# Block sums of a weight matrix: accumulating transfers or VectorE, with a new order of steps

## The chip, the cores and the metric

The kernel runs on one core of one Trainium2 chip. A core has five engines: TensorE (PE in the profile; PEld is its loading of weights), VectorE (DVE), ScalarE (ACT), GpSimd (POOL) and SyncE (SP). Each takes its instructions in order, and they wait for each other by semaphores. SyncE here does nothing but issue transfers (DMA), ScalarE and GpSimd issue some too. The metric is the device time of one execution in microseconds, from repeated runs; the profile comes from one further execution.

## The reference

```python
mod = (_silu(c) @ w_mod).reshape(c.shape[0], 6, 1, -1)
sa, ca, ga, sb, cb, gb = (mod[:, 0], mod[:, 1], mod[:, 2], mod[:, 3], mod[:, 4], mod[:, 5])
h = _layernorm(x, axis=-1) * (1 + ca) + sa
x = x + ga * _A_ref(h, A_w_r, A_w_i)      # irfft2(rfft2(h) * (w_r + 1j * w_i))
h = _layernorm(x, axis=-1) * (1 + cb) + sb
x = x + gb * _B_ref(h, B_w1, B_b1, B_w2)  # mish(h @ w1 + b1) @ w2
```

x is 2048 rows of 512 (float32); w1 is 512 x 1376, w2 is 1376 x 512. The two-dimensional spectral filter (A) comes first, then the dense layer (B).

## The kernel before

The Fourier transforms are products with constant matrices. The forward transform and the filter take up the first part of the program; its order is written out in loops and isn't touched. The change is in the second part, which holds the last transform back to rows (p3_col and p3_row, 16 each, with the addition to x on VectorE at L821) and the dense layer. In this part every piece of work is a *step*: a small function that issues a few instructions. Each step is entered with a key (`plan.at(key, fn, *args)`), the steps are sorted by key and so get a number, and the long string `ORDER` says in which order the numbered steps are issued. There is no scheduler beyond it: each engine gets its instructions in the order in which the steps issue them.

Matrix products of the dense layer are made in parts of lower precision: each operand is split into a high part (a copy with rounding, on ACT) and a low part (the difference, on DVE), and TensorE makes three products of 128x256 for each pair of blocks. For w1 this is `split_w1` (L726 high part, L727 low part).

w1 is taken in block columns t = 1 to 5 of 256 columns each (and a rest of 96, `single_w1`). A block column has four quarters A11, A12, A21, A22, each two k-blocks of 128x128, so 128 partitions x 256 elements. For the first group of 512 rows (i = 0) the products are made plainly from the four quarters (`up`, set PLAIN). For the later three groups (i = 1 to 3) seven products replace eight (a Strassen-Winograd scheme): they need, beside A11, A12 and A22, four sums:

- S1 = A21 + A22
- S3 = A11 - A21
- S2 = A11 - S1
- S4 = A12 + S2

so S2 needs S1, and S4 needs S2. The right operands are sums T1 to T4 of blocks of the activations (`sum_in`, `split_in`). The seven products are named 1 to 7; `up` makes one (L920), `evict` or `plain_evict` (L929) takes it from the bank to SBUF, and `down` (L1023) and its kin multiply by w2 (split at L855, L856).

For each t the raw block column comes by `load_w1` (L716) into `src[t]`, a slot shared with T1 (odd t) or T2 (even t). `block_w1` splits a quarter into a slot of a ring of eight (tile wr), `keep_w1` stores the split to DRAM (L735), and `fetch_w1` (L723) brings it back into the ring for the later row groups. `sum_w1` makes the four sums, in stages called steps 0, 1 and 2:

- S1: step 0 copies A21 from DRAM (L749, SyncE), step 1 adds A22 by an accumulating transfer issued by GpSimd (L752), step 2 splits it and stores the split.
- S3: step 0 negates A21 from `src[t]` (L745, ACT) and adds A11 by an accumulating transfer; step 2 splits and stores.
- S2: step 0 negates S1 in place (L747, ACT) and adds A11 by an accumulating transfer; step 2 splits and stores.
- S4: step 1 adds A12 to S2 by an accumulating transfer; step 2 splits and stores.

The tiles in which sums stand are slots shared with T4 (`temps[0]`), or `wsum` for t = 3; the splits of sums stand in two halves of the slot of T3 before they are stored. The profile calls all of these shared slots hT. SyncE's queue holds, in the order of the steps, the loads of w1 and w2 (L844), the stores of splits, the fetches, and loads for the modulation vector (L619).

Of the kernel before, what the change touches and what calls it, by code (L numbers as in the profile page):

```python
# [10 lines left out]
ALU = mybir.AluOpType  # L11
# [20 lines left out]
POOL_LOW = range(1, 15, 2)  # L32

ORDER = (
# [44 lines left out]
)  # L79


# [1 line left out]
def tile_spectral_block(ctx: ExitStack, tc: tile.TileContext, x_d, w1_d, b1_d, w2_d,  # L83
                        c_d, xt_d, wm_d, wq_d, wz_d, kr_d, km_d, kc_d, ki_d, kf_d, kv_d, kw_d, kp_d, out_d):
    nc = tc.nc
# [615 lines left out]
    ring, raws, src, temps, stage = {}, {}, {}, {}, {}  # L701
# [7 lines left out]
    def w1_block(t, a, v=None):  # L709
        j, i = int(a[1]) - 1, int(a[2]) - 1  # L710
        at = P * j + (256 * t - 256 if v is None else 0)
        return (w1v if v is None else v)[:, 2 * i:2 * i + 2, at:at + P]
# [24 lines left out]
    def sum_w1(t, a, step):  # L737
        if not temps:
            temps[0] = shared("T4").rearrange("p (n k f) -> p n k f", n=4, k=2)
            temps[1] = wsum.rearrange("p (n k f) -> p n k f", n=2, k=2)  # L740
            stage[0] = shared("T3", F32R).rearrange("p (n i k f) -> p n i k f", n=2, i=2, k=2)
        v = temps[1][:, a == "S3"] if t % 3 == 0 else temps[0][:, 2 * (t % 3 - 1) + (a == "S3")]
        if step == 0:
            if a == "S3":
                nc.scalar.mul(v, w1_block(t, "A21", src[t]), -1.0)  # L745
            if a == "S2":
                nc.scalar.mul(v, v, -1.0)  # L747
            if a == "S1":
                nc.sync.dma_start(v, w1_block(t, "A21"))  # L749
                return  # L750
        if step < 2:
            nc.gpsimd.dma_start(v, w1_block(t, {"S1": "A22", "S2": "A11", "S3": "A11", "S4": "A12"}[a]), accum_op=ALU.add)  # L752
            return
        n = stage[1] = stage.get(1, 0) + 1
        w = stage[0][:, n % 2]
        split_w1(w, v)
        keep_w1(t, a, w)
# [349 lines left out]
                fn, args = steps[k]  # L1107
                fn(*args)

    S_KEYS = ((1, -5, 1 / 3), (2, 4, 1.7), (3, 11, 1.5), (4, 18, 1.4), (5, 26, 1.1))  # L1110
    plan = Plan()
    for n in range(N2):
        last = n == N2 - 1
# [45 lines left out]
    for b, key in (("B11", -6.6), ("B21", -5.6), ("B12", -0.5), ("B22", 0.6)):  # L1159
        plan.at(key, split_in, b)  # L1160

    for t, key in ((1, -15.3), (2, -13.5), (3, -3.9), (4, 5), (5, 12.6)):
        plan.at(key, load_w1, t)
    QUARTERS = ("A11", "A12", "A21", "A22")
    for t, keys in ((1, (-9.4, -8.4, -6.4, -5.4)), (2, (-3.4, -2.4, -1.4, -0.4)), (3, (6, 8, 10, 12)),
                    (4, (17, 19, 21, 23)), (5, (26, 28, 30, 32))):
        for a, key in zip(QUARTERS, keys):
            plan.at(key, block_w1, t, a)
            if a != "A21":
                plan.at(key + (0.8 if key < 0 else 1.6), keep_w1, t, a)  # L1170
    for t, key, scale in S_KEYS:
        for a, step, at in (("S1", 0, 0), ("S3", 0, 0.5), ("S1", 1, 2.2), ("S3", 2, 4), ("S1", 2, 5.5), ("S2", 0, 5.9),
                            ("S2", 2, 9), ("S4", 1, 9.6), ("S4", 2, 12.6)):
            plan.at(key + scale * at, sum_w1, t, a, step)

    first_odd = odd[1]
# [25 lines left out]
    for k, (i, t, j) in enumerate(units):  # L1202
# [6 lines left out]
        if (i, t) in PLAIN:  # L1209
            f, e = int(j[0][1]) - 1, int(j[1][2]) - 1  # L1210
            at, half = plain_place(t, f, e)
# [10 lines left out]
    for b in range(NB):  # L1222
        for t in DOWN if b < NB - 1 else (1, 2, 3, 4, 5, 0):
            if b == 0:
                key = dict(zip(DOWN, (12.5, 20.5, 28.5, 33, 40.5, 48.5)))[t] + 0.25
# [16 lines left out]
        at = key if b < NB - 1 else start[b, 3]  # L1242
# [209 lines left out]
```

## Time and profile before

| | |
|---|---|
| median of three runs | 410.33 us (406.42 to 411.56) |
| the profiled execution: time, span | 411.89 us, 409.7 us |
| mean granted TensorE clock | 0.973 |
| busy: PE, DVE, ACT, POOL | 378.2, 299.5, 254.8, 89.4 us |
| moved by DMA | 84.88 MB in 51160 packets |

How to read the rows. Busy time of PE counts pipelined matmuls, so the number of matmuls in a stretch says more than its busy time. A row of a stretch gives its length, then for PE, PEld, DVE, ACT and POOL the busy time and (x) the instructions, then the granted TensorE clock, the share of busy DMA engines, and GB/s. A row of waits gives who waited for whom, the total, the number of waits and the longest. A row of a group gives line, engine, operation, out<-in, shapes and count, then busy time and the mean duration in ns, then the idle time before. In rows of the order of time, the idle time before an instruction and what ended it stand in square brackets. A row of transfers gives what moved, by whose queue, how often, KB each, and the median time from issue to landing.

### The profile page before, as it was taken

The page shows a single profiled execution, that of the slowest core. Times are in us where ns is not written, and L with a number is a line of the kernel's source. Part 1 is how long each engine was busy: PE and PEld are TensorE (multiplying, and loading weights), DVE is VectorE, ACT ScalarE, POOL GpSimd, SP SyncE. Part 2 cuts the span into 40 slices and gives each one's busy share as a digit, 9 for nine tenths or more (in the row PEclk, how much of TensorE's full clock was granted, in tenths as well). Part 3 has the DMA queues.
Part 4 walks back from the last instruction along what each step waited for, and adds up shares of the span by engine and source line. Part 5 has one row for each costly group of instructions (what it writes and reads, how often), then busy time and mean ns, then how long its engine had stood idle before and what let it go on. Part 6 is the DMA issues. An engine that isn't in the chain of part 4 may idle for free.

```text
span 409.7 us, 8223 instructions
## 1 busy us (share of the span) xinstructions
PE 378.2 (92%) x2916; PEld 358.9 (88%) x2916; DVE 299.5 (73%) x732; ACT 254.8 (62%) x563; POOL 89.4 (22%) x122
## 2 busy tenths in 40 slices
PE   7999999989989499498779999999999999999995
PEld 6999867779989498497779999999999999999994
DVE  1898888887798476584468736977548887469896
ACT  1798789975756475496356665655765654354660
POOL 0588567871312121322110000000000000000000
PEclk9999999999999799699889999999999999999999
DMA  8999997788777428486957847676564796837423
GB/s 250 322 330 383 347 333 230 182 323 223 166 209 217 98 65 250 111 240 166 275 132 260 213 136 225 181 181 204 146 195 126 237 272 181 263 72 248 137 40 116
DMA packets 51160, 84.88 MB, mean 207 GB/s; under 512 B 7184, under 2 KB 18800, under 8 KB 50864
## 3 DMA queue, kind: packets, MB, share of 16 engines
q1 hardware_dynamic: 42512, 71.11, 53.1%
q0 software_dynamic: 6448, 6.29, 10.8%
q10 hardware_dynamic: 2160, 6.95, 5.7%
q8 instruction: 23, 0.38, 0.4%
q14 instruction: 17, 0.14, 0.1%
HBM read 67.30 MB, written 13.37 MB: 197 GB/s over the span
## 4 chain that ended last, share of the span: by engine, by line
PE 41%; DVE 4%; DMA 3%; ACT 3%; issue 2%; DVEq 0%; ACTq 0%
PE bank L1023 19%; PE bank L920 17%; PE bank L969 2%; PE bank L1019 2%; DMA buf<-in_B_w_dram 1%; DMA hT<-in_B_w_dram 1%; ACT ah L855 1%; DVE al L856 1%; PE bank L774 1%; DMA wr<-w_A 1%; PE bank L1035 1%; DVE buf L993 1%; DVE x L1080 0%; DVE hT L800 0%; ACT hcr L799 0%
## 5 line engine op out<-in xcount | busy, mean ns | idle before, releaser
L920 PE MATMUL bank<-hB,wr 128*128 128x256 f32 x300 | 46.9, 297 | 9.6 <-ACT buf L929 5.2
L920 PE MATMUL bank<-hT,wr 128*128 128x256 f32 x360 | 52.2, 285 | 1.1 <-DVE scb L945 0.7
L920 PEld LDWEIGHTS bank<-hB,wr 128*128 128x128 f32 x300 | 41.4, 202 | 10.7 <-ACT buf L929 5.4
L920 PEld LDWEIGHTS bank<-hT,wr 128*128 128x128 f32 x360 | 47.0, 192 | 1.6 <-DVE scb L945 0.9
L1075 POOL DMA_DIRECT2D x<-modr x7 | 6.1, 873 | 182.7 <-DVE buf L993 53.2
L752 POOL DMA_DIRECT2D hT<-in_B_w_dram x16 | 19.7, 1230 | 72.6 <-issue 26.0
L1023 PE MATMUL bank<-w2a,ah 128*128 128x256 f32 x161 | 35.5, 285 | 0.0
L1023 PE MATMUL bank<-w2b,ah 128*128 128x256 f32 x147 | 33.5, 291 | 0.8 <-ACT ah L855 0.8
L856 DVE TENSOR_TENSOR al<-buf,ah 128x512 fp32r<-128x512 f32 (+1 forms) x45 | 30.0, 670 | 5.3 <-ACT ah L855 4.8
L855 ACT CAST ah<-buf 128x512 fp32r<-128x512 f32 (+1 forms) x45 | 26.8, 603 | 8.3 <-PE bank L1023 3.6
L920 PE MATMUL bank<-hcr,wr 128*128 128x256 f32 x210 | 30.7, 285 | 0.0
L920 PEld LDWEIGHTS bank<-hcr,wr 128*128 128x128 f32 x210 | 27.7, 194 | 0.1
L1023 PEld LDWEIGHTS bank<-w2a,ah 128*128 128x128 f32 x161 | 27.1, 194 | 0.0
L808 PE MATMUL bank<-kc,d 128*128 128x128 f32 x128 | 25.8, 285 | 0.5 <-ACT d L441 0.5
L1023 PEld LDWEIGHTS bank<-w2b,ah 128*128 128x128 f32 x147 | 25.3, 197 | 1.1 <-ACT ah L855 1.0
L809 PE MATMUL bank<-kc,d 128*128 128x128 f32 x128 | 25.5, 282 | 0.0
L726 ACT CAST hT<-hT 128x256 fp32r<-128x256 f32 x16 | 6.5, 404 | 30.0 <-DMA hT<-in_B_w_dram 20.7
L818 PE MATMUL bank<-kiv,buf 128*128 128x128 f32 x128 | 18.0, 288 | 7.3 <-ACT buf L811 5.7
L818 PEld LDWEIGHTS bank<-kiv,buf 128*128 128x128 f32 x128 | 16.3, 200 | 8.3 <-ACT buf L811 6.5
L1023 PE MATMUL bank<-w,ah 128*128 128x256 f32 x112 | 22.0, 288 | 1.0 <-ACT buf L1046 1.0
L172 DVE BATCH_NORM_STATS2 st<-x 128x6 f32<-128x512 f32 x32 | 21.9, 684 | 0.1
L727 DVE TENSOR_TENSOR hT<-hT,hT 128x256 fp32r<-128x256 f32 x16 | 6.8, 424 | 20.7 <-ACT hT L726 20.7
(290 smaller groups left out, 1142.2 us busy)
## 6 DMA issues: line engine op xcount, KB each, us to landing
wr<-w_S SPq DMA_DIRECT2D x60, 256.0 KB, 3.1
wr<-w_A SPq DMA_DIRECT2D x45, 256.0 KB, 3.2
w_S<-hT SPq DMA_DIRECT2D x20, 256.0 KB, 2.6
x<-in_A_x_dram SPq DMA_DIRECT2D x16, 256.0 KB, 5.0
xring<-in_x_t_dram SPq DMA_DIRECT2D x16, 256.0 KB, 4.6
w_A<-wr SPq DMA_DIRECT2D x15, 256.0 KB, 3.8
x<-modr POOLq DMA_DIRECT2D x7, 512.0 KB, 5.8
out_dram<-x SPq DMA_DIRECT2D x7, 512.0 KB, 4.9
```

Of the source, the lines that this page charges most:

```text
L172: nc.vector.bn_stats(t, x[:, n, :])
L727: nc.vector.tensor_tensor(w[:, 1], r, plain(w[:, 0]), op=ALU.subtract)
L752: nc.gpsimd.dma_start(v, w1_block(t, {"S1": "A22", "S2": "A11", "S3": "A11", "S4": "A12"}[a]), accum_op=ALU.add)
L808: nc.tensor.matmul(o, dj[:, 0:128], kc[0][:, n, :], start=True, stop=False)
L809: nc.tensor.matmul(o, dj[:, 64:192], kc[1][:, n, :], start=False, stop=True)
L818: nc.tensor.matmul(px[:, j * P:(j + 1) * P], e[:, j * P:(j + 1) * P], kiv[:, j, :], start=True, stop=True)
L855: nc.scalar.copy(h, r)
L856: nc.vector.tensor_tensor(l, r, plain(h), op=ALU.subtract)
L920: nc.tensor.matmul(o, w[:, p, k, :], h[:, q, k, :], start=(first and n == 0), stop=(last and n == 5), skip_group_check=True)
L969: nc.tensor.matmul(o, w1s[:, p, k, :], slots[f"B{k // 2 + 1}{s + 1}"][:, q, k % 2, :], start=(u == 0 and m == 0), stop=(m == 11), skip_gro ...
L1019: nc.tensor.matmul(out_ps[b][n][:, 256 * d:256 * d + 256], a[p][:FL, half], w2[0][q][:FL, 256 * d:256 * d + 256], start=False, stop=False, ...
L1023: nc.tensor.matmul(out_ps[b][n][:, 256 * half:256 * half + 256], a[p][:, e], w2[t][q][:, r], start=(t == 1 and half == 0 and i == 0), stop ...
```

## The change

All four sums of a block column are made by VectorE from the raw block column `src[t]`, which stands in SBUF already: one `tensor_tensor` each, of 128 x 256 elements. The copies of A21, the negations and the accumulating transfers are gone: per t, one instruction on DVE for each sum takes the place of one copy by SyncE, two negations by ACT and four transfers issued by GpSimd. S2 and S4 are made in place (in the tile of S1, as before). `src[t]` is now read until S4 is summed.

With this, the keys of the sums and of `load_w1` for t = 3 to 5 are others, there is one step less for each t (1150 instead of 1155), and `ORDER` is written anew: nearly all steps of the second part change places. The steps' own instructions, other than those named, are the same.

```diff
 ORDER = (
-    "3-4 71 0-1 16 21 2 15 14 5-7 73 38 47 8 12 9 62 13 10 69 86 17 24 84 52 19 79 11 26 126 95 18 22 32 23 87 27 "
...
+    "3 1 4 2 0 16 5 21 6 15 7 26 12 73 32 75 71 38 11 9-10 8 14 13 18 52 113 80 17 82 19 22-23 47 20 24 28 105 27 "
...
         if step == 0:
-            if a == "S3":
-                nc.scalar.mul(v, w1_block(t, "A21", src[t]), -1.0)
-            if a == "S2":
-                nc.scalar.mul(v, v, -1.0)
-            if a == "S1":
-                nc.sync.dma_start(v, w1_block(t, "A21"))
-                return
-        if step < 2:
-            nc.gpsimd.dma_start(v, w1_block(t, {"S1": "A22", "S2": "A11", "S3": "A11", "S4": "A12"}[a]), accum_op=ALU.add)
+            block = {k: w1_block(t, k, src[t]) for k in ("A11", "A12", "A21", "A22")}
+            p, q, op = {"S1": (block["A21"], block["A22"], ALU.add), "S3": (block["A11"], block["A21"], ALU.subtract),
+                        "S2": (block["A11"], v, ALU.subtract), "S4": (block["A12"], v, ALU.add)}[a]
+            nc.vector.tensor_tensor(v, p, q, op=op)
             return
         n = stage[1] = stage.get(1, 0) + 1
         w = stage[0][:, n % 2]
...
-    S_KEYS = ((1, -5, 1 / 3), (2, 4, 1.7), (3, 11, 1.5), (4, 18, 1.4), (5, 26, 1.1))
+    S_KEYS = ((1, -5, 1 / 3), (2, 4, 0.7), (3, 13, 0.7), (4, 24, 0.7), (5, 33, 0.7))
...
-    for t, key in ((1, -15.3), (2, -13.5), (3, -3.9), (4, 5), (5, 12.6)):
+    for t, key in ((1, -15.3), (2, -13.5), (3, -2.9), (4, 8.4), (5, 17.4)):
         plan.at(key, load_w1, t)
...
-        for a, step, at in (("S1", 0, 0), ("S3", 0, 0.5), ("S1", 1, 2.2), ("S3", 2, 4), ("S1", 2, 5.5), ("S2", 0, 5.9),
-                            ("S2", 2, 9), ("S4", 1, 9.6), ("S4", 2, 12.6)):
+        for a, step, at in (("S1", 0, 0), ("S3", 0, 0.5), ("S3", 2, 1), ("S1", 2, 2), ("S2", 0, 3),
+                            ("S2", 2, 4), ("S4", 0, 5), ("S4", 2, 6)):
             plan.at(key + scale * at, sum_w1, t, a, step)
```

The order of the changed program puts the sums and splits of t = 1 and 2 and the first of t = 3 among the p3 steps, and the rest among the products of the first row group (i = 0), the last of them just as the second row group begins.

85 rows, old and new, of the table ORDER are left out of this document.

## The prediction

> **What bounds the kernel now.** I read the page first, then busy time and matmul counts by stretch, then the waits of the matrix engine, then the order of time on the engine named there.
>
> ```profile
> PE 378.2 (92%) x2916; PEld 358.9 (88%) x2916; DVE 299.5 (73%) x732; ACT 254.8 (62%) x563; POOL 89.4 (22%) x122
> ```
>
> TensorE (PE) is busy for 378 of 409.7 us: nothing can gain much over 31 us, and a gain must come from stretches in which PE does less than elsewhere. In the stretches, the column after "PE" gives its busy time and the count of matmuls:
>
> ```profile
> 110.00:120.00 10.00, 8.54 (x75) 8.17 (x74) 9.05 (x21) 5.05 (x13) 1.74 (x2) 1.00 0.68 184
> 120.00:130.00 10.00, 9.82 (x86) 9.45 (x85) 8.23 (x21) 6.35 (x14) 1.89 (x2) 1.00 0.87 232
> 130.00:140.00 10.00, 4.45 (x41) 4.21 (x38) 4.78 (x12) 3.27 (x10) 2.43 (x2) 0.91 0.43 96
> 140.00:150.00 10.00, 9.89 (x65) 9.89 (x66) 7.08 (x19) 7.38 (x16) 1.21 (x1) 0.75 0.26 83
> 150.00:160.00 10.00, 10.00 (x86) 10.00 (x85) 9.15 (x29) 9.09 (x20) 2.44 (x2) 1.00 0.76 192
> 160.00:170.00 10.00, 4.75 (x34) 4.55 (x33) 2.96 (x9) 2.38 (x7) 2.44 (x2) 0.78 0.67 195
> 170.00:180.00 10.00, 8.84 (x68) 8.54 (x68) 8.03 (x20) 8.66 (x21) 2.44 (x2) 0.88 0.72 203
> 180.00:190.00 10.00, 10.00 (x87) 10.00 (x86) 5.17 (x15) 6.96 (x16) 2.44 (x2) 1.00 0.69 183
> 190.00:200.00 10.00, 5.76 (x44) 5.17 (x43) 6.45 (x11) 6.12 (x14) 1.22 (x1) 0.98 0.66 183
> 200.00:210.00 10.00, 7.71 (x46) 7.10 (x47) 4.19 (x11) 4.73 (x11) 2.44 (x2) 0.84 0.74 220
> 210.00:220.00 10.00, 10.00 (x73) 10.00 (x72) 6.87 (x18) 4.44 (x10) 0.00 (x0) 0.83 0.73 226
> sum 110.00, PE 89.75 PEld 87.07 DVE 71.97 ACT 64.43 POOL 20.68; mean PE 8.16 PEld 7.92 DVE 6.54 ACT 5.86 POOL 1.88
> ...
> 240.00:250.00 10.00, 10.00 (x87) 10.00 (x86) 4.58 (x14) 6.02 (x15) 0.00 (x0) 1.00 0.56 163
> 220.00:397.00 177.00, 174.68 (x1441) 173.04 (x1440) 132.16 (x324) 104.82 (x221) 6.00 (x7) 1.00 0.64 182
> ```
>
> A full stretch does 86 or 87 matmuls in 10 us (240 to 250). From 110 to 220 us the eleven counts sum to 705 where 946 would fit: 241 missing, 28.0 us. Of these 20.25 us are idle (110 less 89.75); the other 7.8 us are matmuls run at a lower granted clock (0.75 to 0.91 around the idle spells). From 220 to 397 us only 2.3 us are idle. So whatever is to be had lies between 110 and 220 us, and it is about 28 us.
>
> The waits of PE in those 110 us, which sum to that idle time:
>
> ```profile
> PE bank L818 <- ACT buf L811: 5.7, 1, 5.7
> PE bank L920 <- ACT buf L929: 5.2, 1, 5.2
> PE bank L920 <- DMA wr<-w_A: 2.6, 1, 2.6
> PE bank L920 <- ACT wr L726: 1.7, 1, 1.7
> PE bank L1023 <- DVE al L856: 1.5, 2, 0.9
> PE bank L818 <- DVE x L821: 1.5, 2, 1.3
> PE bank L774 <- ACT buf L929: 1.2, 1, 1.2
> PE bank L1023 <- ACT ah L855: 0.8, 1, 0.8
> ```
>
> ScalarE (ACT) is named, but its instructions are short. What held it up, in its order of time (last: idle time before the instruction, and who ended it), with PE's two longest waits and the queue of SyncE:
>
> ```profile
> 138.75 0.40 ACT L726 CAST hT<-hT 128x256 fp32r<-128x256 f32 x1 [6.70 <-DMA hT<-in_B_w_dram]
> 167.01 0.41 ACT L726 CAST hT<-wsum 128x256 fp32r<-128x256 f32 x1 [6.79 <-DMA wsum<-in_B_w_dram]
> 191.17 0.41 ACT L726 CAST hT<-hT 128x256 fp32r<-128x256 f32 x1 [3.66 <-issue]
> 200.17 0.40 ACT L726 CAST hT<-hT 128x256 fp32r<-128x256 f32 x1 [2.88 <-DMA hT<-in_B_w_dram]
> 205.76 0.40 ACT L726 CAST hT<-hT 128x256 fp32r<-128x256 f32 x1 [4.82 <-DMA hT<-in_B_w_dram]
> 140.11 2.08 PE L818 MATMUL bank<-kiv,buf 128*128 128x128 f32 x8 [5.67 <-ACT buf L811]
> 168.26 2.93 PE L920 MATMUL bank<-hB,wr 128*128 128x256 f32 x12 [5.25 <-ACT buf L929]
> SPq L735 <- DVE hT L727: 47.8, 11, 7.1
> ```
>
> Each of the five is the split of a finished sum (L726), waiting at the head of ACT's in-order queue for an accumulating transfer. Copies and evictions for PE stand behind it: PE's two long waits end 1.3 to 1.4 us after the first two of these. The fetches of weights (the 2.6 us) stand on SyncE's queue behind stores (L735) of the same late splits.
>
> **The change, part by part.** *Removed.* Five copies of A21 by SyncE, twenty accumulating transfers by GpSimd, ten negations by ACT.
>
> ```profile
> hT<-in_B_w_dram POOLq DMA_DIRECT2D x16, 128.0 KB, 4.7
> wsum<-in_B_w_dram POOLq DMA_DIRECT2D x4, 128.0 KB, 4.3
> hT<-in_B_w_dram SPq DMA_DIRECT2D x5, 512.0 KB, 5.5
> L745 ACT ACTIVATE hT<-hT 128x256 f32<-128x256 f32 x4 | 1.7, 420 | 0.0
> ```
>
> A chain of three dependent transfers of some 4.5 us each, with an ACT step between, becomes a chain of three instructions on one engine. All of PE's waits listed above but the 1.5 us on L821 (an addition on VectorE, untouched) hang on this: 20.2 less 1.5 is 18.7 us. Of the 7.8 us at a low clock I take the same share, 7.2 us. Together 25.9 us go. The ten negations (4.2 us) and GpSimd's issues were not themselves what PE waited for: nothing for them.
>
> The clock deserves a doubt. The stretch from 200 to 210 us has clock 0.84 though none of PE's waits near it exceeds 2.6 us, so I count low clock after short waits too. The Trainium skill (TensorE: Matmul & The Clock Gate, Part 1) says the clock halves only after an idle window of about 3.4 us and recovers after a busy one. By that rule only the two long waits would have cost clock, 1.7 us each, and the sum below would be some 3.8 us less gain; the rows speak against it.
>
> *Added.* Twenty sums on VectorE (DVE), 128x256 in f32, operands in SBUF; the nearest row is an existing difference of that size, and the stages show how full DVE is there:
>
> ```profile
> L852 DVE TENSOR_TENSOR modr<-buf 128x256 f32<-128x256 f32 x8 | 3.3, 416 | 0.7 <-DMA buf<-in_B_w_dram 0.7
> 94.00:110.00 16.00, 16.00 (x145) 16.00 (x144) 12.23 (x32) 11.04 (x28) 3.87 (x3) 1.00 0.76 192
> 110.00:146.00 36.00, 28.70 (x227) 27.71 (x226) 25.82 (x63) 18.05 (x41) 6.06 (x5) 0.91 0.61 163
> 146.00:213.00 67.00, 54.06 (x403) 52.36 (x402) 41.03 (x103) 41.94 (x96) 14.62 (x12) 0.90 0.68 187
> ```
>
> Twenty at 0.416 us are 8.3 us. DVE is busy for 79.1 of the 119 us from 94 to 213 us; with the sums 87.4 us. If 25.9 us leave this stage, 93.1 us remain, and DVE would be 94% busy: this is where the new cost must appear, because DVE also finishes x (L821), whose bank the next p3_row needs, and all low halves. The stretch from 110 to 120 us shows 9.05 of 10, the two from 110 to 130 us 0.864 on average, with PE nearly fed. At 0.94 the sums cost nothing, at 0.864 the stage takes 101.2 us, 8.1 us more. I take the middle, 4 us: the new order stretches the sums of t = 4 and 5 to the end of the stage, where more slack lies.
>
> *Moved.* A block column's raw slot is now read until S4 is summed, so load_w1 of t+2 waits for it, and the new order puts these loads later. Steps between the load and its first reader hold, for t = 3, 44 matmuls (first_in, two p3_col, one p3_row), at 8.7 a microsecond 5.1 us; for t = 5, 34 matmuls, 3.9 us; for t = 4, 96. Landing takes 5.5 us. So t = 3 lacks 0.4 us and t = 5 1.6 us, 2 us in all; the bounds are 0 (DVE late there anyway) and twice the landing, 11 us. Queued behind such a wait on DVE are L821 and the low halves, and PE waits for those. All other steps change places, but with the same instructions: 2916 matmuls, the same splits, stores (L735) and fetches. Counting dependences of PE on ACT and DVE in the two programs that are closer than the time of 1 us of matmuls, I find 49 before and 47 after: the new order is about as tight as the old one. In the old one such tightness cost PE 2.3 us in the 177 us after 220, so nothing is added for it.
>
> *Sum.* -25.9 + 4 + 2 = -19.9 us. The profiled execution has a span of 409.7 us and took 411.9; the median of the three runs is 410.3, so a span of 389.8 us corresponds to about **390 us**. The form's own range: 382 if the remaining 2 us go too and the additions are all hidden; 404 if DVE costs 8.1 and the loads 11 us.
>
> **The rivals.** *VectorE becomes the bound.* For it: 94% of what remains. If the order packs DVE only to 0.80 (the stage from 94 to 110 us had 0.76, unforced), 87.4 us take 109 us, a gain of 10 us: 400 us. Against: 0.864 over 20 us already stands in the rows.
>
> *One landing takes the place of another.* DVE now waits for raw blocks as ACT waited for sums: five loads of 5.5 us are 27.5 us, against 24.9 us that ACT waited in the five rows above. Nothing is gained: 410 us. Against: the loads are issued without any chain, and all but two have ample lead.
>
> *Slower: the raw slots lock.* SyncE's queue is in order: a load that waits for a slot holds up stores and fetches, and it stands behind stores that wait for splits, up to 7.1 us. If for t = 3, 4 and 5 each load comes late by 7.1 and lands in 5.5 us with DVE standing at its first sum, that is 37.8 us: 410.3 - 25.9 + 37.8 = 422 us. The gain is gone from 8.6 us a load on, and the loss is over 2% from 11.4 us. For it: such waits of 47.8 us exist today. Against: most of them were themselves splits waiting for accumulations.
>
> **How the numbers follow.** Forecast 0.65, VectorE 0.16, landing for landing 0.09, locked slots 0.10. A measurement of this kernel tells about 2% from no change: 402 and 418.5 us. Faster: nearly all of the forecast and most of the second case, 0.77; within 2%: 0.13; slower: 0.10. Range 382 to 404, leaving out the locked slots, most of landing for landing, and a little below.
>
> **What would show it.** Right: no line L726 idle on a transfer of w1 over 1 us; PE's counts of 80 and more in every stretch from 100 to 200 us, granted clock 1.0 there; DVE over 0.85 in that stage; the last matmul of the first row group some 20 us earlier. Wrong in size: DVE's sums or L821 among what PE waits for, over 8 us. Wrong in kind: DVE idle before its sums for load_w1 by several us each, or PE waits of new origin after 200 us.

## The result, and the profile after

The changed kernel takes **379.9 us** (median of four runs, 379.27 to 380.36); the kernel before takes 409.94 us beside it (four runs, 406.42 to 411.56). The ratio is 0.928, with a 95% interval of 0.921 to 0.934. The prediction was 390.0 us with a range of 382 to 404: the direction and the place were right, the time lies 2 us below the range. The span went from 409.7 to 378.6 us, 31.1 us less, where 19.9 us less was forecast.

The page after, first its busy times, then five of the ten stretches from 100 to 200 us with the sum of all ten (columns as before: length; busy time and count of PE, PEld, DVE, ACT, POOL; granted clock; share of busy DMA engines; GB/s):

```profile
PE 367.7 (97%) x2916; PEld 351.4 (93%) x2916; DVE 305.0 (81%) x752; ACT 251.4 (66%) x553; POOL 64.8 (17%) x102
```

```profile
110.00:120.00 10.00, 10.00 (x92) 10.00 (x91) 9.51 (x28) 6.63 (x18) 0.00 (x0) 1.00 0.49 183
...
130.00:140.00 10.00, 10.00 (x89) 10.00 (x89) 8.97 (x22) 6.36 (x12) 0.00 (x0) 1.00 0.32 102
140.00:150.00 10.00, 10.00 (x85) 10.00 (x85) 9.76 (x31) 9.37 (x24) 0.00 (x0) 1.00 0.55 174
...
160.00:170.00 10.00, 10.00 (x87) 10.00 (x86) 9.43 (x25) 9.45 (x21) 0.00 (x0) 1.00 0.66 238
...
190.00:200.00 10.00, 10.00 (x86) 10.00 (x85) 9.32 (x25) 5.82 (x13) 0.00 (x0) 1.00 0.80 253
sum 100.00, PE 100.00 PEld 99.97 DVE 93.83 ACT 76.14 POOL 0.00; mean PE 10.00 PEld 10.00 DVE 9.38 ACT 7.61 POOL 0.00
```

In the sum PE has no idle time, the clock is 1.00 throughout, and DVE is busy for 93.83 of 100 us. The first products with the sums of the activations (tile hT), which come where the second row group begins, stand here in before and after; the first p3_col stands ahead of them:

```profile
91.34 0.49 PE L808 MATMUL bank<-kc,d 128*128 128x128 f32 x2 [0.46 <-ACT d L441]
...
213.00 1.26 PE L920 MATMUL bank<-hT,wr 128*128 128x256 f32 x8
```

```profile
90.49 0.49 PE L802 MATMUL bank<-kc,d 128*128 128x128 f32 x2 [0.46 <-ACT d L440]
...
181.73 0.88 PE L914 MATMUL bank<-hT,wr 128*128 128x256 f32 x6
```

From the one to the other, 121.7 us became 91.2 us: 30.5 of the 31.1 us. From there to the end it is 196.7 and 196.9 us. The stage had lost about 30 us, and it lost nothing any more. (Line numbers are one less than before up to about L740, and six less behind: L726 and L727 are now L725 and L726, L735 is L734, L818 is L812, L920 is L914.)

### The profile page after: what moved, and what is told of

Read it like the earlier page. It is cut to its first block, busy times and chain, and to the rows that moved or that the text cites. A ratio compares the mean times of both kernels' runs of the same rounds, so it can differ in the third digit from the quotient of the medians.

```text
span 378.6 us, 8181 instructions
## 1 busy us (share of the span) xinstructions
PE 367.7 (97%) x2916; PEld 351.4 (93%) x2916; DVE 305.0 (81%) x752; ACT 251.4 (66%) x553; POOL 64.8 (17%) x102
## 4 chain that ended last, share of the span: by engine, by line
PE 87%; DVE 5%; DMA 3%; ACT 2%; SPq 1%; issue 1%; DVEq 0%; ACTq 0%
PE bank L914 27%; PE bank L1017 24%; PE bank L802 4%; PE bank L812 4%; PE bank L803 4%; PE bank L547 4%; PE bank L963 3%; PE bank L596 3%; PE bank L302 3%; PE bank L257 3%; PE bank L1013 2%; PE bank L527 2%; PE bank L768 2%; DMA xring<-in_x_t_dram 1%; DMA x<-in_A_x_dram 1%; PE bank L304 1%
## 5 line engine op out<-in xcount | busy, mean ns | idle before, releaser
L914 PE MATMUL bank<-hT,wr 128*128 128x256 f32 x360 | 51.4, 284 | 0.3 <-DVE even L939 0.3
L914 PEld LDWEIGHTS bank<-hT,wr 128*128 128x128 f32 x360 | 46.6, 191 | 0.5 <-DVE even L939 0.5
L914 PE MATMUL bank<-hB,wr 128*128 128x256 f32 x300 | 43.4, 284 | 0.1
L914 PEld LDWEIGHTS bank<-hB,wr 128*128 128x128 f32 x300 | 39.1, 191 | 0.3 <-ACT odd L927 0.3
L1017 PE MATMUL bank<-w2b,ah 128*128 128x256 f32 x147 | 32.4, 284 | 0.0
L914 PE MATMUL bank<-hcr,wr 128*128 128x256 f32 x210 | 30.5, 285 | 0.9 <-DVE odd L943 0.6
L914 PEld LDWEIGHTS bank<-hcr,wr 128*128 128x128 f32 x210 | 27.3, 191 | 1.3 <-DVE odd L943 0.8
L802 PE MATMUL bank<-kc,d 128*128 128x128 f32 x128 | 24.9, 276 | 0.5 <-ACT d L440 0.5
L803 PE MATMUL bank<-kc,d 128*128 128x128 f32 x128 | 24.7, 275 | 0.0
L776 ACT ACTIVATE buf<-bank,cols 128x256 f32<-128x256 f32 x28 | 14.1, 563 | 11.1 <-PE bank L768 11.1
L302 PE MATMUL bank<-buf,mring 128*128 128x512 f32 x48 | 20.7, 430 | 0.5 <-ACT buf L288 0.3
L802 PEld LDWEIGHTS bank<-kc,d 128*128 128x128 f32 x128 | 19.4, 192 | 0.7 <-ACT d L440 0.7
L803 PEld LDWEIGHTS bank<-kc,d 128*128 128x128 f32 x128 | 19.4, 192 | 0.0
L1017 PEld LDWEIGHTS bank<-w,ah 128*128 128x128 f32 x112 | 17.4, 191 | 1.2 <-ACT buf L1040 1.2
```

Source lines behind the costliest of these rows:

```text
L302: nc.tensor.matmul(pa, m[:, a, 0:128], g, start=(i == 0), stop=False)
L776: nc.scalar.activation(dst[:, 256 * e:256 * e + 256], ps[:, 256 * e:256 * e + 256], AF.Identity, bias=cols[:, 1, 0, k:k + 1], scale=cols[: ...
L802: nc.tensor.matmul(o, dj[:, 0:128], kc[0][:, n, :], start=True, stop=False)
L803: nc.tensor.matmul(o, dj[:, 64:192], kc[1][:, n, :], start=False, stop=True)
L914: nc.tensor.matmul(o, w[:, p, k, :], h[:, q, k, :], start=(first and n == 0), stop=(last and n == 5), skip_group_check=True)
L1017: nc.tensor.matmul(out_ps[b][n][:, 256 * half:256 * half + 256], a[p][:, e], w2[t][q][:, r], start=(t == 1 and half == 0 and i == 0), stop ...
```

## The experiments

Times beside a kernel are medians of its runs, and ratios are to the kernel before on the same chip. Line numbers shift with each edit. In the kernels with the old order or with transfers, lines behind L750 are three less than before: L808 is L811 of before, L815 is L818 (p3_row), L818 is L821 (the addition to x), L917 is L920. The late loads keep the lines of the changed kernel, and the kernels with more work on VectorE have one more behind L725.

**The new order without the new sums.** The changed kernel's `ORDER`, with the copies, negations and accumulating transfers of before.

```diff
         if step == 0:
...
-            nc.vector.tensor_tensor(v, p, q, op=op)
+            if a == "S3":
+                nc.scalar.mul(v, w1_block(t, "A21", src[t]), -1.0)
+            if a == "S2":
+                nc.scalar.mul(v, v, -1.0)
+            if a == "S1":
+                nc.sync.dma_start(v, w1_block(t, "A21"))
+            nc.gpsimd.dma_start(v, w1_block(t, {"S1": "A22", "S2": "A11", "S3": "A11", "S4": "A12"}[a]), accum_op=ALU.add)
```

> The new order with the copies, negations and accumulating transfers of before. Theory: the new order by itself is worth nothing; its splits stand 0 to 9 us of matmuls behind their sums, by my count 16 of 20 splits lack together about 50 us of landing (4.5 us for a transfer, 8.5 us for S1's copy and accumulation), of which PE's queue covers 1 to 2 us each, and the clock falls after the waits: 410 to 440 us, slower than before or equal, PE idle behind ScalarE. Rival: the order gives a good part of the gain: below 400 us.

Measured: 439.12 us, ratio 1.072 (1.067 to 1.077). Its waits from 88 to 230 us, PE's and ACT's (total, number, longest):

```profile
PE bank L1020 <- ACT ah L852: 10.4, 1, 10.4
PE bank L815 <- ACT buf L808: 10.3, 3, 4.4
PE bank L917 <- ACT wr L725: 5.7, 1, 5.7
```

```profile
ACT hT L725 <- DMA hT<-in_B_w_dram: 21.1, 6, 6.4
ACT hT L725 <- issue: 18.5, 4, 7.9
```

By itself the order loses 30 us: its splits stand close behind their sums, and with transfers they wait at the head of ACT's queue. (`issue` means that the profile names nothing that ended the wait. The trace's times do: there, too, the split starts 0.02 to 0.06 us after the landing of an accumulating transfer, and so does the one with `issue` in the prediction's rows, at 191.17 us after a landing at 191.11.) The order is made for sums that take 0.42 us.

**The new sums without the new order, three times.** `sum_w1` computes on DVE, and `ORDER` is that of before, save for a few steps that must move because `src[t]` is now read until S4.

```diff
+    S, L = "sum_w1", "load_w1"
+    MOVES = (((L, 3), (S, 1, "S4", 1)), ((S, 2, "S2", 0), (S, 2, "S1", 2)), ((S, 2, "S2", 2), (S, 2, "S2", 0)),
+             ((S, 2, "S4", 1), (S, 2, "S2", 2)), ((L, 4), (S, 2, "S4", 1)), ((L, 5), (S, 3, "S4", 1)),
+             ((S, 3, "S1", 1), (S, 1, "S4", 2)), ((S, 5, "S2", 2), (S, 5, "S2", 0)), ((S, 5, "S4", 1), (S, 5, "S2", 2)))
...
+            for what, behind in MOVES:
+                places.remove(find[what])
+                places.insert(places.index(find[behind]) + 1, find[what])
```

Each entry names a step (function, t, sum, stage) and the step behind which it goes: three loads and six stages of sums.

> The sums by VectorE, the rest in the order of before; only the loads of the raw columns 3, 4 and 5 and seven steps of the sums (S1 of t = 3, S2 and S4 of t = 2 and 5) are moved, which the shared slots force. Theory: the 30 us were the landings of the accumulating transfers at the head of ScalarE's queue, so the sums alone bring nearly all of it whatever the order: 380 to 386 us, no wait of ScalarE's high part over 1 us, matmul counts of 85 to 92 in every 10 us from 100 to 190 us. Rival: the new order is worth a good part, since in the old one evictions and splits stand differently to the p3 steps and products: 392 us or more, with PE waiting for evictions or for x in the stage.

Measured: 389.38 us, ratio 0.950 (0.944 to 0.956). So 20 of the 30 us: the time lies between the two expectations. What PE still waited for:

```profile
PE bank L815 <- ACT buf L808: 3.4, 2, 1.9
PE bank L917 <- DMA wr<-w_A: 2.2, 1, 2.2
PE bank L815 <- DVE x L818: 0.9, 1, 0.9
```

Ahead of the two waits for L808, ACT stands 3.1 us for a result of DVE (L197), which comes behind a sum that waits 1.5 us for its raw column, and 2.7 us at the split of a sum that DVE makes late. Is that the old order, or my moves? In the second kernel the moved steps are spread: S2 and S4 of t = 1 and 2 over more room, the first sums of t = 4 later.

```diff
+    MOVES = (((S, 1, "S2", 0), (S, 1, "S1", 2)), ((S, 1, "S2", 2), (W, 2, "A21")), ((S, 1, "S4", 1), (S, 2, "S1", 0)),
...
+             ((S, 2, "S4", 1), (W, 3, "A12")), ((L, 4), (S, 2, "S4", 1)), ((S, 4, "S3", 0), (W, 3, "A22")),
```

(W is `block_w1`.)

> Sums by VectorE and the old order once more, but the steps that the shared slots force are moved otherwise: t = 1's S2 and S4 earlier, so that the load of column 3 has some 9 us ahead of its reader; t = 2's S2 and S4 spread; the first sums of t = 4 later. In the other kernel of this kind (389.4 us) PE lost 10.2 us in the stage to four events: 0.94 us, 1.47 us, 1.93 us with a spell of half clock, all between 115 and 140 us where the moved steps are crowded, and 2.17 us for a fetch, with a spell, at 187 us. Theory (the old order needs only the room that fast sums give, and what was lost came from the crowding): 382 to 385 us, only the fetch is left. Rival (the old order of p3, evictions and splits is itself what costs 9 us): 387 to 391 us, waits for L808 and x in the same place.

Measured: 390.52 us, ratio 0.953 (0.948 to 0.958). The time looks as if the rival were right; the trace says otherwise. The two waits for L808 are gone, and one new event has come, in the order of time on DVE, ACT and PE:

```profile
149.44 0.43 DVE L749 TENSOR_TENSOR hT<-hT 128x256 f32<-128x256 f32 x1 [2.33 <-DMA hT<-in_B_w_dram]
```

```profile
149.90 0.41 ACT L726 CAST hT<-hT 128x256 fp32r<-128x256 f32 x1 [5.90 <-DVE hT L749]
```

```profile
155.37 1.69 PE L917 MATMUL bank<-hB,wr 128*128 128x256 f32 x12 [3.19 <-ACT buf L926]
```

DVE's first sum of t = 4 waits for its raw column; ACT, which has reached the split of that sum, stands 5.9 us with the evictions behind it; PE stands 3.2 us. The rest was a fetch (2.8 us), which stood on SyncE's queue behind the store of a split that I had moved ahead of it. The third kernel repairs these two: the sums and S3's split of t = 4 go behind quarters of t = 4 that stood ten matmuls or more later, and S2's split of t = 5 stays where it was.

```diff
-             ((S, 2, "S4", 1), (W, 3, "A12")), ((L, 4), (S, 2, "S4", 1)), ((S, 4, "S3", 0), (W, 3, "A22")),
-             ((S, 4, "S1", 1), (S, 4, "S3", 2)), ((L, 5), (S, 3, "S4", 1)), ((S, 5, "S2", 2), (S, 5, "S2", 0)),
-             ((S, 5, "S4", 1), (S, 5, "S2", 2)))
+             ((S, 2, "S4", 1), (W, 3, "A12")), ((L, 4), (S, 2, "S4", 1)), ((S, 4, "S3", 0), (W, 4, "A11")),
+             ((S, 4, "S3", 2), (W, 4, "A12")), ((S, 4, "S1", 1), (W, 4, "A21")), ((L, 5), (S, 3, "S4", 1)),
+             ((S, 5, "S4", 1), (S, 5, "S2", 2)))
```

> Once more the sums by VectorE in the old order, with the forced moves eased after the trace of the second such kernel (390.5 us). There PE lost 3.6 us behind a load of column 4 that came 2.3 us late for its reader, 2.8 us and a spell of half clock for a fetch that stood on SyncE's queue behind a store I had moved ahead of it, 0.7 us for x and 0.3 us for an eviction. Now the sums of t = 4 stand some ten matmuls or more behind that load's old reader, and S2 of t = 5 is left where it was. Theory (the old order loses only where the raw slots are read too late or a store is put ahead of a fetch): 382 to 386 us, no PE wait over 1 us left but perhaps the fetch. Rival (the old order loses some 10 us whatever is moved, each repair opening another wait): 388 to 392 us.

Measured: 384.08 us, ratio 0.933 (0.927 to 0.940). PE's waits left:

```profile
PE bank L771 <- ACT buf L926: 1.8, 1, 1.8
PE bank L815 <- DVE x L818: 0.7, 1, 0.7
```

The time lies in the range of the theory, but one wait over 1 us is left that it didn't have: ACT's split at 153.40 us waits 2.4 us for the store that frees its half of T3's slot, and PE's 1.8 us follow. So the sums bring nearly all of the gain by themselves, if thirteen steps get room for them. What the order written anew adds beyond that is 2 us by the ratios (0.933 and 0.928, whose intervals overlap) and 4 us by the medians and spans (382.2 and 378.6). A careless placing of the same sums costs 5 to 6 us more by the medians.

**One sum of four by transfer.** The changed kernel, but S4 is made by the accumulating transfer.

```diff
+            if a == "S4":
+                nc.gpsimd.dma_start(v, w1_block(t, "A12"), accum_op=ALU.add)
+                return
             nc.vector.tensor_tensor(v, p, q, op=op)
```

> As the changed kernel, but S4 = A12 + S2 is made by the accumulating transfer of before (five of 128 KB). By the positions, the splits of S4 lack 1.3, 1.4, 0, 1.9 and 3.1 us of a landing of 4.5 us. Theory (each landing that the order does not cover stands at the head of ScalarE's queue and passes to PE): 383 to 390 us, ScalarE waits at its high part of S4 by about 8 us in all, PE by 2 to 6 us. On the clock: if short waits cost clock, as I read the rows of before, stretches with a granted clock under 1.0 appear around PE waits of 1 to 3 us; if only an idle window of 3.4 us does, the clock stays at 1.00. Rival: PE has enough issued ahead and nothing shows: 380 us.

Measured: 391.07 us, ratio 0.954 (0.949 to 0.959): 11 us more for five transfers, over the upper bound of what I expected. ACT's waits from 88 to 230 us, and PE's longest:

```profile
ACT hT L725 <- DMA hT<-in_B_w_dram: 5.6, 2, 2.9
...
ACT hT L725 <- issue: 5.2, 1, 5.2
```

```profile
PE bank L917 <- ACT hT L796: 4.7, 1, 4.7
```

```profile
190.00:200.00 10.00, 8.86 (x53) 8.64 (x54) 8.79 (x23) 6.10 (x13) 0.00 (x0) 0.67 0.58 162
...
sum 140.00, PE 132.32 PEld 130.59 DVE 109.61 ACT 95.18 POOL 8.71; mean PE 9.45 PEld 9.33 DVE 7.83 ACT 6.80 POOL 0.62
```

Three of the five splits wait, 10.8 us in all, and the last of them passes 4.7 us to PE. (It is the one with `issue`: its transfer lands at 190.10 us, and it starts at 190.17.) The sum is over 90 to 230 us: PE is idle for 7.7 us, in the changed kernel for 0.5. The stretch that holds the end of the long wait has a clock of 0.67. PE starts again at 191.14 us and runs at half clock until 196.5, which is some 2.7 us more. The 7.2 and 2.7 us are most of the 11 us. What short waits cost, this kernel doesn't decide: its one spell of half clock stands at the wait of 4.7 us, and its other waits, of 0.8 us at most, have none.

**Raw columns 3 and 5 loaded as late as possible**, directly ahead of the step that first reads them. This speaks to the prediction's +2 us for the loads.

```diff
+    MOVES = ((3, ("sum_w1", 3, "S3", 0)), (5, ("block_w1", 5, "A11")))
...
+            for t, ahead in MOVES:
+                places.remove(find["load_w1", t])
+                places.insert(places.index(find[ahead]), find["load_w1", t])
```

> As the changed kernel, but the raw columns 3 and 5 are loaded directly ahead of the step that first reads them, so that nothing lies between issue and reader. Theory (a late raw column costs as the prediction's term for the loads had it): VectorE or ScalarE stand for about 4 us each at the first reader, PE has 1 to 2 us of work ahead, so PE loses about 2.5 us each: 384 to 388 us. Rival: the stage has slack enough that late loads cost nothing: 380 to 381 us, and then the term could not have been seen in any order.

Measured: 387.2 us, ratio 0.946 (0.942 to 0.950), 7.3 us more. But one load alone does it. Column 3 costs nothing, though nothing stands between it and its reader in the order. Its issue and its reader, then those of column 5 (this kernel), with PE behind:

```profile
125.41 0.42 SPq L715 DMA_DIRECT2D hT<-in_B_w_dram  x1
```

```profile
130.11 0.42 DVE L746 TENSOR_TENSOR wsum<-hT 128x256 f32<-128x256 f32 x1
```

```profile
159.28 0.42 SPq L715 DMA_DIRECT2D hT<-in_B_w_dram  x1
```

```profile
164.04 0.40 ACT L725 CAST wr<-hT 128x256 fp32r<-128x256 f32 x1 [6.75 <-DMA hT<-in_B_w_dram]
```

```profile
164.91 0.51 PE L1017 MATMUL bank<-w2a,ah 128*128 128x256 f32 x2 [3.99 <-ACT ah L849]
```

For column 3 SyncE has nothing to wait for, runs ahead of DVE and issues the load 4.7 us before its reader comes up there. For column 5 the load stands behind a store and two loads of w2 that go out from 156.49 us on; it is issued at 159.28 us, when ACT has been waiting for 2 us already. Of PE's loss 4.0 us are idle and 3.4 us are half clock.

**More work for VectorE**, against the prediction's +4 us. Low halves of w1 are computed twice (only the twenty quarters; then all forty) or three times.

```diff
-    def split_w1(w, r):
+    def split_w1(w, r, low=1):
         nc.scalar.copy(w[:, 0], r)
-        nc.vector.tensor_tensor(w[:, 1], r, plain(w[:, 0]), op=ALU.subtract)
+        for _ in range(low):
+            nc.vector.tensor_tensor(w[:, 1], r, plain(w[:, 0]), op=ALU.subtract)
...
-        split_w1(ring[t, a], w1_block(t, a, src[t]))
+        split_w1(ring[t, a], w1_block(t, a, src[t]), 2)
```

This is the first of the three. In the others the last two lines stay as they were, and `low` is 2 or 3 for all.

> As the changed kernel, but the low half of each of the twenty quarters of w1 is computed twice: 20 more VectorE instructions of 0.42 us, 8.4 us. In the changed kernel VectorE is busy for 85.3 of the 92 us from 90 to 182 us. Theory (VectorE costs nothing until it is full): 93.6 us of work in a stage of 91.5, so about 2 us more, 382 us. Rival (the prediction's term: near full, the order of work costs as if the engine held only 0.93 of the stage): 93.6/0.93 = 100.7, 9 us more, 389 us.

> As the changed kernel, but all forty low halves of w1 (quarters and sums) are computed twice: 16.8 us more of VectorE, 102 us in the stage. Theory (nothing until full): 10.5 us more, 390 us. Rival (0.93 is all that fits): 109.7, 18 us more, 398 us. Below 385 us VectorE's work can be put off past the stage.

> As the changed kernel, but all forty low halves are computed three times: 33.6 us more of VectorE, 119 us in the stage. Theory (nothing until full): 27 us more, 407 us. Rival (0.93): 128, 36 us more, 416 us. Between the three kernels the step from 40 to 80 more instructions should be the full 16.8 us under both.

| more on DVE | time, us | ratio to before | over 379.9, us | not paid, us |
|---|---|---|---|---|
| 8.4 us | 386.04 | 0.942 (0.937 to 0.947) | 6.1 | 2.3 |
| 16.8 us | 394.72 | 0.963 (0.958 to 0.969) | 14.8 | 2.0 |
| 33.6 us | 412.97 | 1.007 (1.004 to 1.010) | 33.1 | 0.5 |

The stage of the changed kernel, and of the three, each to where its second row group begins or up to 2 us behind it:

```profile
90.00:182.00 92.00, 91.54 (x792) 91.48 (x792) 85.28 (x222) 69.52 (x156) 1.44 (x1) 1.00 0.60 200
```

```profile
90.00:188.00 98.00, 94.98 (x803) 93.42 (x804) 94.08 (x245) 70.52 (x158) 1.07 (x1) 1.00 0.56 189
```

```profile
90.00:197.00 107.00, 97.46 (x801) 94.67 (x800) 102.14 (x265) 70.52 (x156) 1.54 (x1) 0.98 0.53 174
```

```profile
90.00:216.00 126.00, 104.51 (x797) 101.48 (x797) 119.75 (x307) 71.16 (x157) 1.46 (x1) 0.92 0.44 149
```

DVE is busy for 0.927 of the stage in the changed kernel and 0.960, 0.955 and 0.950 where it is loaded further. In the last two it waits for other engines or transfers for no more than 1.9 us in the whole stage; the rest of what it lacks are gaps between its instructions. So it fills to about 0.955 here, and work beyond comes out in the time: from the second kernel to the third, 16.8 us of work cost 18.3 us. The times lie between theory and rival. By the medians some 2 us are free, not 6 and not 0; by the spans of the profiled executions (383.3, 392.8 and 411.8 us, against 378.6) it is 3.7, 2.6 and 0.4 us. The changed kernel stands 2 to 4 us from being bound by VectorE.

## Why the prediction was right and wrong

*Right.* PE was the bound, the loss lay between 110 and 220 us, and the cause was the accumulating transfer at the head of ACT's in-order queue: S4 alone by transfer brings 11 us of it back, and the old order with DVE's sums shows 20 to 27 us of gain. The signs named beforehand all came: no L725 waits for a transfer of w1, counts of 85 to 92 in every stretch from 100 to 200 us at clock 1.00, DVE over 0.85, the second row group 31 us earlier, where the forecast had some 20 for the end of the first. No new wait after 200 us. What the change does merely by having fewer transfers wasn't run by itself; of PE's waits before, only the 2.6 us for a fetch is put down to a DMA directly.

*Wrong in size*, by 11.2 us of span, in four steps. The first was the largest. The second alone explains why the time fell below the range: its lower end of 382 us already had the additions at nothing and all of the 28.0 us gone.

1. *"At 0.94 the sums cost nothing, at 0.864 the stage takes 101.2 us ... I take the middle, 4 us."* They cost 0: PE isn't idle from 100 to 200 us, with DVE busy for 0.94. The 0.864 was no ceiling. In those 20 us of the kernel before, DVE was idle for 2.7 us, behind a transfer (1.6 us) and behind ACT's half of a split (1.5 us) that itself waited for an accumulating transfer. The loaded kernels put the ceiling at 0.95 to 0.96. The rival "VectorE becomes the bound" was 2 to 4 us away all the same: with twenty instructions more it began to hold.
2. *The yardstick of 86 matmuls in 10 us.* It came from 240 to 250 us. The stage also holds p3 steps, whose matmuls are shorter: 91 and 92 fit there (110 to 120 us after). The row from 94 to 110 us in the prediction said so already, with 145 in 16 us. With 28.0 us I had the loss 2.5 us too small. It also shows when the stretch is counted in one piece: 110 to 220 us holds 684 matmuls and not 705 (one that reaches over the border of two rows is counted in both), and at the 8.64 a microsecond of the whole stage after (788 in 91.2 us) 30.8 us are missing. The idle part was right, 20.3 us. The rest isn't all clock: 67 matmuls start in the spells of half clock, which costs some 7 us, and some 3 us are time in which PE counts as busy and isn't full. (The last matmul ahead of a wait is on record with 0.28 us, where matmuls in a row start 0.12 us apart.)
3. *"So t = 3 lacks 0.4 us and t = 5 1.6 us, 2 us in all."* They lack nothing. I measured the lead in matmuls from the load's place in the order, but SyncE reaches that place ahead of the others:

```profile
124.52 0.43 SPq L715 DMA_DIRECT2D hT<-in_B_w_dram  x1
...
151.63 0.42 SPq L715 DMA_DIRECT2D hT<-in_B_w_dram  x1
```

```profile
131.12 0.42 DVE L746 TENSOR_TENSOR wsum<-hT 128x256 f32<-128x256 f32 x1
```

```profile
158.17 0.42 ACT L725 CAST wr<-hT 128x256 fp32r<-128x256 f32 x1
```

   The leads are 6.6 and 6.5 us instead of 5.1 and 3.9, and the landing takes 4.3 us at the median instead of 5.5. Had a load been late, its price would have been more than the lack: 7.3 us for column 5.

```profile
hT<-in_B_w_dram SPq DMA_DIRECT2D x5, 512.0 KB, 4.3
```

4. *"All but the 1.5 us on L821", and 0.6 us of clock* were left standing, 2.1 us. They went too. The wait for x is a matter of the order: 0.7 to 0.9 us of it stand in all three kernels with DVE's sums in the old one.

These are 4.0 + 2.5 + 2.0 + 2.1 = 10.6 us, which with the 19.9 make the 30.5 us of the stage; the rest came before 91 us, in steps that the change does not touch. That *"nothing is added"* for the new order was nearly right as a term (the new order brings 2 to 4 us), but not shown by the reason given. A count of close dependences over the whole program, 49 and 47, says little of an order: with the sums in the old one, the time went from 384 to 390 us with the places of some thirteen steps. (The count wasn't made for those kernels.) What the traces show there are single loads, stores and sums that come late for a reader at the head of a queue.

*The clock.* I let 7.2 of 7.8 us go with the waits, by the rows and against the rule of the Trainium skill (TensorE: Matmul & The Clock Gate, Part 1). They went: the clock is 1.00 in all stretches shown. The other reading would have put the time 3.8 us further from the result.

*The rivals.* Landing for landing (410 us) did not come, since the two tight loads have 2 us to spare over a landing of 4.3 us. The locked slots (422 us) would need every late load to cost some 12 us; one that came as late as ACT's 6.75 us cost 7.3.

## What to carry to other kernels

Where an engine's in-order queue serves a busy TensorE, look for the instruction at its head that waits for a transfer: its cost is what stands behind it, and it is bought back by computing the same thing from data already on the chip, as long as the engine that takes it over isn't full (VectorE was at about 0.95 of this stage). Take the yardstick of a full stretch from the same mix of work, and an engine's ceiling from a stretch in which it is the bound, not from one in which it waits. Judge whether a load is early by when its queue issues it, not by its place in the written order.

## What the runs showed that had not been expected

A short wait of PE can cost more than itself. In stretches of 1 us, behind the wait of 1.81 us in the eased old order (first), and around the wait of 3.99 us with the late loads (second):

```profile
154.00:155.00 1.00, 0.00 (x0) 0.00 (x0) 0.94 (x3) 1.00 (x4) 0.00 (x0) 1.00 0.93 305
155.00:156.00 1.00, 0.94 (x5) 0.95 (x6) 0.91 (x3) 1.00 (x4) 0.00 (x0) 0.58 1.02 380
156.00:157.00 1.00, 1.00 (x7) 1.00 (x7) 0.96 (x4) 1.00 (x4) 0.00 (x0) 0.50 0.39 88
157.00:158.00 1.00, 1.00 (x6) 1.00 (x6) 1.00 (x5) 1.00 (x4) 0.00 (x0) 0.50 0.98 250
158.00:159.00 1.00, 1.00 (x8) 1.00 (x7) 0.70 (x2) 1.00 (x3) 0.00 (x0) 0.71 0.58 219
```

```profile
165.00:166.00 1.00, 0.91 (x4) 0.70 (x5) 0.79 (x2) 1.00 (x4) 0.00 (x0) 0.69 0.00 0
...
171.00:172.00 1.00, 1.00 (x6) 1.00 (x6) 1.00 (x4) 0.94 (x3) 0.00 (x0) 0.50 0.06 21
172.00:173.00 1.00, 1.00 (x10) 1.00 (x9) 1.00 (x4) 0.00 (x0) 0.00 (x0) 0.90 0.00 0
```

The clock is halved for about 3.4 us in the first and 6.8 us in the second, with PE at work all the while: 1.7 and 3.4 us lost beside the waits. Yet a wait of 3.19 us, in the spread old order, was followed by none:

```profile
155.00:156.00 1.00, 0.63 (x5) 0.63 (x6) 0.97 (x4) 1.00 (x4) 0.00 (x0) 1.00 0.00 0
156.00:157.00 1.00, 1.00 (x10) 1.00 (x10) 1.00 (x4) 1.00 (x4) 0.00 (x0) 1.00 0.69 262
```

So the length of the wait alone does not decide. The granted clock changes on a grid: its spells of half clock last 3.41 us or a multiple, and within a run they start whole multiples of 3.41 us apart (in the kernel before, the later three 8, 18 and 21 steps after the first). Here are two steps of that grid in the eased old order, then two in the spread one, counted back from its spell at 187.90 us:

```profile
151.75:155.16 3.41, 1.60 (x14) 1.39 (x13) 3.05 (x9) 1.76 (x5) 0.00 (x0) 1.00 0.76 220
155.16:158.58 3.42, 3.42 (x17) 3.42 (x18) 3.06 (x10) 3.42 (x10) 0.00 (x0) 0.50 0.79 247
```

```profile
150.35:153.77 3.42, 1.83 (x16) 1.63 (x14) 2.20 (x10) 3.35 (x5) 0.00 (x0) 1.00 0.63 196
153.77:157.18 3.41, 1.81 (x15) 1.81 (x15) 3.35 (x11) 3.41 (x11) 0.00 (x0) 1.00 0.52 193
```

The wait of 1.81 us lies in one step and leaves it more than half idle; the wait of 3.19 us falls on a border and leaves 1.6 us in each. In all eleven traces, without their first 12 and last 8 us, the 21 steps at full clock with 1.81 us or more of idle PE are followed by half clock; of the eight with 1.41 to 1.80 us, one is (1.58 us, in the kernel before). This is read from the traces, and no run tested it by moving a wait. Why some spells last one step and some two stays open. The Trainium skill (TensorE: Matmul & The Clock Gate, Part 1) tells of a free-running activity window of about 3.4 us; the lengths of the spells agree with it. That it takes a whole idle window, as the same part has it, does not agree with a spell behind a wait of 1.81 us.
